# Moving side splits, side sums and weight sums to other places of a hand-written order in a fused attention and bilinear-GLU kernel

## The chip, the cores and the metric

The kernel runs on one core of a Trainium2 chip. A core has a matrix engine (PE, whose weight loads the profile lists apart as PEld), a vector engine (DVE), a scalar engine (ACT), GpSimd (POOL) and a queue engine (SP) that issues the DMA transfers. Each engine works through its own instructions in the order in which the program issues them, and semaphores make one wait for another. The metric is the device time of one execution in microseconds. A difference of 0.2%, about 1.07 us here, is the smallest that is called a difference.

## The reference, cut to what matters

```python
mod = (silu(c) @ w_mod).reshape(1, 6, 1, -1)          # shifts, scales and gates sa, ca, ga, sb, cb, gb
h = layernorm(x) * (1 + ca) + sa
x = x + ga * linear_attention(h, A_wqkv, A_wo)
h = layernorm(x) * (1 + cb) + sb
g = h @ B_w_gate                                       # 2048 x 512 by 512 x 1376
u = h @ B_w_up
x = x + gb * ((g * u) @ B_w_down)                      # 2048 x 1376 by 1376 x 512
```

All tensors are float32. The change is in the last three lines: the feed-forward part behind the second layer norm.

## The kernel before, in words

**Precision.** A float32 operand is split in two parts, a high part `h` (the value rounded to the matrix engine's format) and a low part `l = x - h`. A product is three matrix products: `h*h`, `h*l` and `l*h`. The helper `split` does it: ACT writes `h` (line 202), and DVE, or POOL where `low` names it, writes `l` (line 203). So every low part is a DVE instruction behind an ACT instruction.

**Chunks and sides.** The 2048 tokens are cut in four chunks of 512. The gate and up projections of two chunks at a time are done by a Strassen-Winograd scheme with seven products in place of eight. The 2x2 block matrix on the left has the two chunks as rows and the two halves of the 512 features as columns. Its sides are the blocks `a11`, `a12` (first chunk of the pair), `a21`, `a22` (second chunk) and the sums `s1 = a21 + a22`, `s3 = a11 - a21`, `s2 = s1 - a11`, `s4 = a12 - s2` (`Left.sum`, line 1059, on DVE). Each half of the features is two tiles of 128 rows, so each side comes twice, for `k` = 0 and 1. The seven products use `a11, s1, s2, a12, s3, s4, a22`, each split in `h` and `l`.

**Steps and places.** One call of `block` is one step: one tile of 128 columns of gate and up for one pair of chunks. Steps 0 to 7 work on the first and second chunk, steps 8 to 18 on the third and fourth. A step has seven products of six matmuls each (`times`, line 1150), 42 matmuls of 128x512, and after each product a place where other work is put in: `p1` behind the product of `a11`, then `p5` (`s1`), `p6` (`s2`), `p2` (`a12`), `p7` (`s3`), `p3` (`s4`) and `p4` (`a22`), in this order. The four accumulators `a, b, c, d` are PSUM banks; steps from 3 on take the set named `bank` when they are even and the set named `acc` when odd. In each step ACT copies `a` to `b` behind the first product, `d` to SBUF behind the second, and `b` to `c` and to SBUF behind the third (line 1155). At the fifth product DVE adds accumulator `c` to a copy (line 1212), and the seventh product then adds on to the same `c`. So **the last six matmuls of a step may not start before the L1212 instruction of that step has read `c`**, and between the fifth and the seventh product lies only the sixth, six matmuls. L1216 and two L1178 follow on DVE in the same step.

**What sets the order around it.** The order is written out by hand. Two tables fill the places of the steps. One is the dictionary near the end of the main function: it holds the work on the third and fourth chunk that steps 8 and later need, namely `flips` (DVE block transposes, line 344, into the one buffer `wide`), `turned` (ACT, line 349, makes a block from `wide`), `sums` and `split_in`. The other is `Down.planned`: the weights of the down projection, in pairs `i` of row tiles. For each even step 8, 10, 12, 14 and 16 it scales the pair by `gb` (`w_scale`, line 1326, two DVE instructions), makes the four Winograd sums `t1` to `t4` (`w_sum`, line 1340, four DVE instructions of 128x256, both inputs in SBUF) and splits the parts (`w_parts`, lines 1318 and 1319). POOL has its own load in steps 2 to 11: at `p4` of a step it makes four sums of the next gate and up weights (line 1094), and at `p7`, behind four ACT instructions (lines 1105 and 1108), the four low parts of the next step's weights (line 1112). All DMAs named here are issued by SP.

## Time and profile before

| what | value |
|---|---|
| median of 3 runs | 536.81 us (536.5 to 537.18) |
| the profiled execution, device time | 537.02 us |
| its span, first to last instruction | 535.3 us |
| granted matrix clock | 1.00 of full speed, throughout |
| moved by DMA | 113.41 MB, mean 212 GB/s |

Between the span and the device time of the same execution lie 1.7 us at the ends. The steps 3 to 18 stand in the span from 282.28 us on, at some 9.5 us each. In the rows below a row gives its start in us from the start of the span, its length in us, the engine, the line, the instruction, output<-inputs, the size, and in square brackets how long the engine had been idle before it and for whom it had waited. A row that ends in x2 is two instructions that follow each other without a gap.

### The profile page before, as it was taken

Reading aid. Unit: us, or ns where it says so; the run is one execution under the profiler, and the core shown is the slowest. Engines: PE = TensorE matmul, PEld = TensorE weight load, DVE = VectorE, ACT = ScalarE, POOL = GpSimd, SP = SyncE. Lnnn points to the kernel's source line nnn. Section 1 sums busy time; section 2 is a strip of 40 time slices with the busy share of each in tenths; the row PEclk is TensorE's granted clock in tenths of the full one; section 3 lists DMA queues with packets and bytes.
Section 4 is the critical chain, followed back from the end, with each engine's and each line's share of the span. In section 5 each row is a group of like instructions: output and inputs, shape, how many; then the busy total and the mean of one; then the engine's idle time right before and its main releaser. Section 6 shows DMA issues by size and latency. Waiting matters only on the chain.

```text
span 535.3 us, 8162 instructions
## 1 busy us (share of the span) xinstructions
PE 527.9 (99%) x2551; PEld 440.9 (82%) x2551; DVE 416.4 (78%) x732; ACT 312.3 (58%) x588; POOL 143.3 (27%) x141
## 2 busy tenths in 40 slices
PE   8999999999999999999999999999999999999997
PEld 7888888888878878878888878678888889998887
DVE  7997879999999888779645697777477677788594
ACT  3696878759577774576584853563424454425530
POOL 2001010000012220076587894591001244100000
PEclk9999999999999999999999999999999999999999
DMA  8912426220065155957979965297999789969866
GB/s 276 387 45 79 158 95 212 89 79 2 32 209 182 55 202 156 282 164 212 297 246 308 334 258 149 82 337 254 370 334 326 257 313 335 290 226 278 254 158 153
DMA packets 102203, 113.41 MB, mean 212 GB/s; under 512 B 26448, under 2 KB 57168, under 8 KB 102160
## 3 DMA queue, kind: packets, MB, share of 16 engines
q1 hardware_dynamic: 97808, 111.85, 63.9%
q10 hardware_dynamic: 4352, 1.05, 0.9%
q8 instruction: 20, 0.33, 0.3%
q14 instruction: 23, 0.19, 0.1%
HBM read 70.91 MB, written 41.94 MB: 211 GB/s over the span
## 4 chain that ended last, share of the span: by engine, by line
PE 96%; DVE 1%; POOL 1%; DMA 1%; issue 0%; ACT 0%; POOLq 0%
PE bank L1150 17%; PE acc L1150 14%; PE acc L882 8%; PE acc L1413 6%; PE bank L216 4%; PE bank L217 4%; PE bank L215 4%; PE acc L1434 4%; PE bank L1434 4%; PE bank L1413 3%; PE acc L424 3%; PE acc L423 3%; PE acc L422 3%; PE bank L967 2%; PE bank L965 2%; PE bank L966 2%
## 5 line engine op out<-in xcount | busy, mean ns | idle before, releaser
L1150 PE MATMUL bank<-h,w 128*128 128x512 f32 x462 | 107.3, 390 | 2.1 <-DVE u L1212 2.1
L1150 PEld LDWEIGHTS bank<-h,w 128*128 128x128 f32 x462 | 86.5, 188 | 21.3 <-DVE u L1212 3.4
L1150 PE MATMUL acc<-h,w 128*128 128x512 f32 (+1 forms) x336 | 77.8, 390 | 0.0
L1150 PEld LDWEIGHTS acc<-h,w 128*128 128x128 f32 (+1 forms) x336 | 61.9, 184 | 14.6 <-DVE u L1212 0.3
L271 POOL TENSOR_TENSOR rstd<-ve,half 128x2 f32<-128x2 f32 (+3 forms) x13 | 11.9, 912 | 108.7 <-DVE ve L270 45.7
L1155 ACT ACTIVATE bank<-bank 128x512 f32<-128x512 f32 x24 | 14.0, 582 | 46.1 <-PE bank L1150 41.5
L215 PE MATMUL bank<-w,h 128*128 128x512 f32 x104 | 40.6, 391 | 0.0
L217 PE MATMUL bank<-w,h 128*128 128x512 f32 x104 | 40.6, 390 | 0.0
L216 PE MATMUL bank<-w,h 128*128 128x512 f32 x104 | 40.5, 390 | 0.0
L882 PE MATMUL acc<-w,xh 128*128 128x512 f32 x120 | 37.4, 392 | 0.0
L1155 ACT ACTIVATE acc<-acc 128x512 f32<-128x512 f32 (+1 forms) x18 | 10.5, 581 | 42.8 <-PE acc L1150 31.4
L1413 PE MATMUL acc<-w,kh 128*128 128x256 f32 (+1 forms) x176 | 31.9, 283 | 0.0
L1112 POOL TENSOR_TENSOR w<-raw,w 128x256 fp32r<-128x256 f32 (+3 forms) x22 | 24.6, 1118 | 24.6 <-ACT w L1105 24.6
L1112 POOL TENSOR_TENSOR w<-t,w 128x512 fp32r<-128x512 f32 (+1 forms) x22 | 31.1, 1415 | 0.0
L1413 PEld LDWEIGHTS acc<-w,kh 128*128 128x128 f32 (+1 forms) x176 | 27.6, 192 | 0.2
L882 PEld LDWEIGHTS acc<-w,xh 128*128 128x128 f32 x120 | 22.4, 188 | 5.1 <-DVE w L793 0.3
L422 PE MATMUL acc<-kh,xh 128*128 128x512 f32 x64 | 25.1, 392 | 0.0
L424 PE MATMUL acc<-kl,xh 128*128 128x512 f32 x64 | 25.0, 390 | 0.0
L423 PE MATMUL acc<-kh,xl 128*128 128x512 f32 x64 | 24.9, 390 | 0.0
L1413 PE MATMUL acc<-w,kl 128*128 128x256 f32 x88 | 24.9, 283 | 0.0
L202 ACT ACTIVATE kh<-u 128x512 fp32r<-128x512 f32 (+1 forms) x38 | 21.0, 623 | 5.6 <-PE acc L1413 3.0
L203 DVE TENSOR_TENSOR kl<-u,kh 128x512 fp32r<-128x512 f32 (+1 forms) x28 | 17.6, 685 | 7.8 <-ACT kh L202 7.8
(267 smaller groups left out, 1342.0 us busy)
## 6 DMA issues: line engine op xcount, KB each, us to landing
right<-w SPq DMA_DIRECT2D x49, 256.0 KB, 3.2
w<-right SPq DMA_DIRECT2D x49, 256.0 KB, 5.1
w<-down_t SPq DMA_DIRECT2D x36, 256.0 KB, 5.3
w<-down_b SPq DMA_DIRECT2D x27, 256.0 KB, 4.6
raw<-in_w_mod_dram SPq DMA_DIRECT2D x24, 256.0 KB, 4.2
down_t<-w SPq DMA_DIRECT2D x20, 256.0 KB, 4.7
x<-in_A_x_dram SPq DMA_DIRECT2D x16, 256.0 KB, 5.4
x<-x SPq DMA_DIRECT2D x16, 256.0 KB, 4.4
```

The lines of the kernel that those rows point to most:

```text
L215: nc.tensor.matmul(ps, ah, bh, start=i == 0, stop=False)
L216: nc.tensor.matmul(ps, ah, bl, start=False, stop=False)
L217: nc.tensor.matmul(ps, al, bh, start=False, stop=i == n - 1)
L422: nc.tensor.matmul(tacc[k], xh[:, a:b], kh, start=first, stop=False)
L423: nc.tensor.matmul(tacc[k], xl[:, a:b], kh, start=False, stop=False)
L424: nc.tensor.matmul(tacc[k], xh[:, a:b], kl, start=False, stop=last)
L882: nc.tensor.matmul(yps[i], x, y, start=False, stop=k == KD - 1 and x is al, skip_group_check=True)
L1112: sub = lambda out, x, y: (on or nc.gpsimd).tensor_tensor(out, x, f32(y), op=ALU.subtract)
L1150: mm = lambda x, y, **kw: nc.tensor.matmul(ps, x[:, k], y, skip_group_check=True, **kw)
L1155: nc.scalar.activation(out, x, AF.Copy)
L1413: nc.tensor.matmul(ps, x[:, a:b], y, start=start, stop=False, skip_group_check=True)
L1434: nc.tensor.matmul(ps, of[:, x], y, start=start, stop=False, skip_group_check=True)
```

## The change

Part one is in `Down.planned`: the sums `t1, t2` go from place `p2` to `p5` of the even steps, and `t3, t4` from `p3`, where they stood behind the splits of `b11` and `b21`, to `p6`. Part two is the dictionary: the splits of the third chunk's `a11` (both `k`) and of its `a12` for `k` = 0 go into step 3, beside the flips of the fourth chunk; `turned` of the fourth chunk moves one place or more ahead in step 4; and the sums and the splits of the sums, which stood in steps 5 to 7, are spread over steps 4 to 7. The split of the second `a22` goes from `p6` to `p1` of step 8. No instruction is added or taken away, and SP and POOL keep the order of what they do; their buffers come in another turn.

```diff
-                put(a, "p2", lambda i=i: self.w_sum(i, "t1", "t2"))
-                put(a, "p3", lambda i=i: self.w_parts(i, "b11", "b21"), lambda i=i: self.w_sum(i, "t3", "t4"))
+                put(a, "p5", lambda i=i: self.w_sum(i, "t1", "t2"))
+                put(a, "p6", lambda i=i: self.w_sum(i, "t3", "t4"))
+                put(a, "p3", lambda i=i: self.w_parts(i, "b11", "b21"))
                 put(a, "p4", lambda i=i: self.w_parts(i, "b22", "t1"))
...
-        (3, "p1"): [turned(1, 2, "a12")], (3, "p6"): [flips(3, 0)], (3, "p2"): [flips(3, 1)],
-        (3, "p3"): [flips(3, 2)], (3, "p4"): [flips(3, 3)],
-        (4, "p5"): [turned(0, 3, "a21"), split_in(0, "a11")], (4, "p6"): [split_in(0, "a12")], (4, "p2"): [turned(0, 3, "a22")],
-        (4, "p3"): [turned(1, 3, "a21"), split_in(1, "a11")], (4, "p4"): [turned(1, 3, "a22")],
-        (5, "p1"): [sums(0, "s1")], (5, "p5"): [split_in(1, "a12")], (5, "p6"): [sums(0, "s3")], (5, "p2"): [split_in(0, "s1")],
-        (5, "p3"): [sums(1, "s1")], (5, "p4"): [split_in(0, "s3"), sums(1, "s3")],
-        (6, "p1"): [sums(0, "s2")], (6, "p5"): [split_in(1, "s1")], (6, "p2"): [split_in(0, "s2"), sums(1, "s2")],
-        (6, "p3"): [split_in(1, "s3")], (6, "p4"): [sums(0, "s4")],
-        (7, "p1"): [split_in(1, "s2")], (7, "p6"): [sums(1, "s4")], (7, "p2"): [split_in(0, "s4")],
-        (7, "p3"): [split_in(1, "s4")], (7, "p4"): [split_in(0, "a22")], (8, "p6"): [split_in(1, "a22")]}.items():
+        (3, "p1"): [turned(1, 2, "a12")], (3, "p5"): [split_in(0, "a11")], (3, "p6"): [flips(3, 0)],
+        (3, "p2"): [flips(3, 1), split_in(0, "a12")], (3, "p3"): [flips(3, 2)], (3, "p4"): [flips(3, 3), split_in(1, "a11")],
+        (4, "p1"): [turned(0, 3, "a21")], (4, "p5"): [turned(0, 3, "a22")], (4, "p6"): [split_in(1, "a12"), sums(0, "s1")],
+        (4, "p2"): [turned(1, 3, "a21"), sums(0, "s3")], (4, "p3"): [turned(1, 3, "a22")],
+        (4, "p4"): [split_in(0, "s1"), sums(1, "s1")],
+        (5, "p5"): [sums(1, "s3")], (5, "p6"): [split_in(0, "s3")], (5, "p2"): [sums(0, "s2")],
+        (5, "p3"): [split_in(1, "s1")], (5, "p4"): [sums(1, "s2")],
+        (6, "p1"): [split_in(0, "s2")], (6, "p6"): [sums(0, "s4")], (6, "p2"): [split_in(1, "s3")], (6, "p4"): [split_in(1, "s2")],
+        (7, "p1"): [sums(1, "s4")], (7, "p5"): [split_in(0, "s4")], (7, "p2"): [split_in(1, "s4")],
+        (7, "p4"): [split_in(0, "a22")], (8, "p1"): [split_in(1, "a22")]}.items():
```

The order on DVE shows where this matters. A row is the line, the instruction, output<-inputs and the size. The first place is step 4 up to its last accumulator read; `f` are blocks of the third and fourth chunk, `s` sums, `h` low or high parts, and L1212 reads accumulator `c` (`bank_2883`). Before:

```order
L203 TENSOR_TENSOR h_3413<-f_3269,h_3412 128x512
L203 TENSOR_TENSOR h_3426<-f_3279,h_3425 128x512
L1212 TENSOR_TENSOR u_3408<-bank_2883,u_3408 128x512
L1216 TENSOR_TENSOR u_3423<-bank_2884,u_3423 128x512
L1178 TENSOR_TENSOR u_3423<-bank_2881,u_3423 128x512
```

And in the changed kernel:

```order
L203 TENSOR_TENSOR h_3404<-f_3294,h_3403 128x512
L203 TENSOR_TENSOR h_3436<-f_3303,h_3435 128x512
L1059 TENSOR_TENSOR s_3439<-f_3414,f_3424 128x512
L1059 TENSOR_TENSOR s_3463<-f_3269,f_3414 128x512
L1212 TENSOR_TENSOR u_3422<-bank_2883,u_3422 128x512
```

The two splits ahead of L1212 are those of another `k`, and two sums of sides have come in between them and L1212.

The second place is DVE between the last accumulator read of step 5 (`acc_3183`) and L1212 of step 6 (`bank_2883`). Before:

```order
L1178 TENSOR_TENSOR u_3523<-acc_3183,u_3523 128x512
L203 TENSOR_TENSOR h_3610<-s_3538,h_3609 128x512
L1059 TENSOR_TENSOR s_3613<-f_3294,f_3487 128x512
L1059 TENSOR_TENSOR s_3622<-s_3515,f_3269 128x512
L203 TENSOR_TENSOR h_3633<-s_3594,h_3632 128x512
L203 TENSOR_TENSOR h_3666<-s_3622,h_3665 128x512
L1059 TENSOR_TENSOR s_3669<-s_3594,f_3294 128x512
L1212 TENSOR_TENSOR u_3630<-bank_2883,u_3630 128x512
```

And in the changed kernel:

```order
L1178 TENSOR_TENSOR u_3535<-acc_3183,u_3535 128x512
L1059 TENSOR_TENSOR s_3621<-s_3520,f_3294 128x512
L203 TENSOR_TENSOR h_3631<-s_3572,h_3630 128x512
L1059 TENSOR_TENSOR s_3651<-f_3279,s_3572 128x512
L203 TENSOR_TENSOR h_3674<-s_3537,h_3673 128x512
L1212 TENSOR_TENSOR u_3640<-bank_2883,u_3640 128x512
```

Six side instructions stood there, four stand there now; the others have gone to steps 4, 5 and 7.

The third place is DVE in step 10, the second step with weight sums; `raw` are the weights of the down projection, `row_1578` is `gb`, `t` holds the sums, `w` their low parts. Before:

```order
L1326 TENSOR_TENSOR raw_4004<-raw_4004,row_1578 128x512
L1340 TENSOR_TENSOR t_4054<-raw_4002 128x256
L1340 TENSOR_TENSOR t_4054<-raw_4004,t_4054 128x256
L1212 TENSOR_TENSOR u_4029<-bank_2883,u_4029 128x512
L1216 TENSOR_TENSOR u_4038<-bank_2884,u_4038 128x512
L1178 TENSOR_TENSOR u_4038<-bank_2881,u_4038 128x512
L1319 TENSOR_TENSOR w_4088<-raw_4002,w_4088 128x256
L1319 TENSOR_TENSOR w_4091<-raw_4004,w_4091 128x256
L1340 TENSOR_TENSOR t_4055<-raw_4004,raw_4002 128x256
L1340 TENSOR_TENSOR t_4055<-raw_4004,t_4054 128x256
```

And in the changed kernel:

```order
L1326 TENSOR_TENSOR raw_4004<-raw_4004,row_1578 128x512
L1340 TENSOR_TENSOR t_4031<-raw_4002 128x256
L1340 TENSOR_TENSOR t_4031<-raw_4004,t_4031 128x256
L1340 TENSOR_TENSOR t_4032<-raw_4004,raw_4002 128x256
L1340 TENSOR_TENSOR t_4032<-raw_4004,t_4031 128x256
L1212 TENSOR_TENSOR u_4029<-bank_2883,u_4029 128x512
```

The two sums that stood behind L1212 and the splits now stand ahead of L1212. The same holds in steps 8, 12, 14 and 16.

## The prediction

> **What bounds the kernel now.** The first view is the page, busy time by engine.

> ```profile
> PE 527.9 (99%) x2551; PEld 440.9 (82%) x2551; DVE 416.4 (78%) x732; ACT 312.3 (58%) x588; POOL 143.3 (27%) x141
> ```

> PE is busy for 99% of the span and so the bound almost everywhere, and the change takes no matmul away. It can only gain where PE waits, and only lose by making PE wait. The second view is busy time by stretch, cut at the first matmul of each step (steps 3, 4, 5, 6, 8, 10 and 11; first the stretch, its length, then each engine's busy time with its count).

> ```profile
> 282.28:291.80 9.52, 9.52 (x44) 7.88 (x43) 3.99 (x7) 4.85 (x9) 7.53 (x9) 1.00 0.92 320
> 291.80:301.33 9.53, 9.53 (x44) 7.87 (x42) 5.32 (x9) 7.20 (x14) 6.26 (x8) 1.00 1.03 348
> 301.33:311.05 9.72, 9.72 (x44) 7.81 (x43) 8.37 (x11) 6.92 (x14) 9.64 (x9) 1.00 0.98 340
> 311.05:322.13 11.08, 9.82 (x44) 7.80 (x42) 11.05 (x13) 5.81 (x11) 11.00 (x9) 1.00 0.52 198
> 331.65:342.32 10.67, 9.82 (x44) 7.78 (x42) 8.00 (x13) 5.56 (x13) 4.46 (x5) 1.00 0.02 8
> 351.98:361.80 9.82, 9.82 (x43) 7.81 (x42) 7.76 (x12) 6.37 (x14) 9.74 (x9) 1.00 1.00 344
> 361.80:371.32 9.52, 9.52 (x43) 7.88 (x42) 6.83 (x14) 3.21 (x7) 1.71 (x2) 1.00 0.66 233
> ```

> A step without a wait is 9.52 us at a granted clock of 1.00. Step 6 loses 1.56, step 8 loses 1.15, step 10 loses 0.30, step 5 loses 0.20. The timeline of PE names the cause in the two longest:

> ```profile
> 320.63 1.66 PE L1150 MATMUL bank<-h,w 128*128 128x512 f32 x6 [1.26 <-DVE u L1212]
> 340.82 1.66 PE L1150 MATMUL bank<-h,w 128*128 128x512 f32 x6 [0.85 <-DVE u L1212]
> ```

> It is the last product of the step, six matmuls, waiting for L1212. L1212 in steps 5 and 6, the two low parts ahead of it in step 6, a low part with POOL idle, and a row of POOL for later:

> ```profile
> 308.81 0.68 DVE L1212 TENSOR_TENSOR u<-acc,u 128x512 f32<-128x512 f32 x1
> 316.45 2.37 DVE L203 TENSOR_TENSOR h<-s,h 128x512 fp32r<-128x512 f32 x2
> 319.90 0.68 DVE L1212 TENSOR_TENSOR u<-bank,u 128x512 f32<-128x512 f32 x1
> 333.08 0.68 DVE L203 TENSOR_TENSOR h<-f,h 128x512 fp32r<-128x512 f32 x1
> 299.14 0.74 POOL L1112 TENSOR_TENSOR w<-raw,w 128x256 fp32r<-128x256 f32 x1 [1.28 <-ACT w L1105]
> ```

> In step 6 DVE is busy for 11.05 of 11.08 us and POOL for 11.00 (the row by stretch), and a low part that takes 0.68 alone takes 2.37/2, about 1.2, there: the two take turns. L1212, whose one input is in PSUM, keeps its 0.68.

> **A rule for one step.** The last product is due 36 of 42 matmuls into the step, 9.52 x 36/42 = 8.16. Loss = (end of L1212) - (start of step + 8.16) + 0.19 fits all four: step 5, 309.49 - 309.49 + 0.19 = 0.19 (0.20 in the row); step 6, 320.58 - 319.21 + 0.19 = 1.56; step 8, 340.77 - 339.81 + 0.19 = 1.15; step 10, 360.26 - 360.14 + 0.19 = 0.31 (0.30). The ends of steps 8 and 10 come from rows below. So L1212 has to start by 7.29 into the step.

> **The change part by part.** *Step 6.* Two of six side instructions leave, about 2.4 us. The last one left ahead of L1212 is a low part behind an ACT high part; that comes behind two ACT copies, about 5.9 into the step, and even at 1.2 is over at about 7.1. Then L1212 waits for its own accumulator only. **-1.56.**

> *Step 8.* Here the wait was a DVE gap:

> ```profile
> 333.21 0.58 ACT L1155 ACTIVATE bank<-bank 128x512 f32<-128x512 f32 x1 [4.16 <-PE bank L1150]
> 337.56 0.69 DVE L203 TENSOR_TENSOR h<-f,h 128x512 fp32r<-128x512 f32 x1 [2.60 <-ACT h L202]
> 340.09 0.68 DVE L1212 TENSOR_TENSOR u<-bank,u 128x512 f32<-128x512 f32 x1
> 337.86 0.86 POOL L1112 TENSOR_TENSOR w<-raw,w 128x192 fp32r<-128x192 f32 x1 [8.04 <-ACT w L1105]
> ```

> DVE sat 2.60 us for the high part of the second `a22`, which stood at `p6`. At `p1` it follows the copy at 333.21, 3 us earlier, and then the low part and all four weight sums run in a stretch where POOL is idle until 337.86: about 334.4 + 0.6 + 4 x 0.35 = 336.4, long before L1212 can start at 338.7. **-1.15.** The bound on the other side is nothing gained.

> *Step 10.* The same edit meets another neighbour:

> ```profile
> 354.79 1.35 DVE L203 TENSOR_TENSOR kl<-u,kh 96x512 fp32r<-96x512 f32 x2 [1.80 <-ACT kh L202]
> 356.06 1.82 DVE L1326 TENSOR_TENSOR raw<-raw,row 128x512 f32<-128x512 f32 x2
> 357.81 0.96 DVE L1340 TENSOR_TENSOR t<-raw 128x256 f32<-128x256 f32 x1
> 358.81 0.85 DVE L1340 TENSOR_TENSOR t<-raw,t 128x256 f32<-128x256 f32 x1
> 359.58 0.68 DVE L1212 TENSOR_TENSOR u<-bank,u 128x512 f32<-128x512 f32 x1
> 361.78 2.01 DVE L1319 TENSOR_TENSOR w<-raw,w 128x256 fp32r<-128x256 f32 x2
> 363.71 0.41 DVE L1340 TENSOR_TENSOR t<-raw,raw 128x256 f32<-128x256 f32 x1
> 354.95 2.39 POOL L1094 TENSOR_TENSOR t<-raw,raw 128x256 f32<-128x256 f32 x1
> 359.34 1.47 POOL L1112 TENSOR_TENSOR w<-t,w 128x512 fp32r<-128x512 f32 x1
> 360.77 1.30 POOL L1112 TENSOR_TENSOR w<-raw,w 128x512 fp32r<-128x512 f32 x1
> ```

> DVE starts late because its first low parts wait for high parts behind the first product, and L1212 has no slack (0.30 lost). Two more L1340 now come at 359.58. POOL then holds a 128x512 low part from about 359.5 to 360.76. The third sum waits for it and ends reading at 361.1; POOL's next one has taken the turn, to 362.2; the fourth sum is over at 362.56, and L1212 ends at 363.24 in place of 360.26. **+2.98.** That a short DVE instruction waits out a long POOL one is in the row at 361.78: two instructions that take 0.41 each alone (363.71) took 2.01, as POOL's 128x512 at 360.77 and the next ran. Bounds: 0.70 (two at 0.35 without a wait) and 2.98; I take the upper, to which that row is nearest.

> *Steps 12, 14, 16.* DVE waits for PE before L1212 there; the smallest gap of the three:

> ```profile
> 416.47 0.69 DVE L1212 TENSOR_TENSOR u<-bank,u 128x512 f32<-128x512 f32 x1 [1.76 <-PE bank L1150]
> ```

> Two sums of 0.35 fit into 1.76: **0**. Without that cover it would be 0.7 for each.

> *Step 4.* The rows that time ACT and POOL there (the first is the copy behind the third product, one step earlier):

> ```profile
> 286.56 0.58 ACT L1155 ACTIVATE acc<-acc 128x512 f32<-128x512 f32 x1 [0.76 <-PE acc L1150]
> 298.65 0.41 ACT L1105 ACTIVATE w<-raw 128x256 fp32r<-128x256 f32 x1
> ```

> Now a low part and two sums stand ahead of L1212. The low part needs its ACT high part behind the two copies of the third product; the first of these comes 4.28 into a step (286.56 in the step that starts at 282.28), so at 296.08, and the high part, two ACT instructions later at 0.5 each, is done by 297.67. Low part to 298.3, first sum to 298.9, at 0.6 each. ACT's L1105 comes about 0.38 earlier than at 298.65, since one instruction less holds up the third product's copies, and POOL's L1112 0.49 behind it as before (299.14), at 298.76; so the second sum waits until 299.48 and is over at 300.05; L1212 ends at 300.73. Loss 300.73 - 299.96 + 0.19 = 0.96 against 0.01: **+0.95**. Bounds: +0.40 if the second sum meets no POOL instruction, +0.95.

> *Step 5.* Five side instructions stand ahead of L1212 where four stood; by the same count, taking turns with POOL, the last sum starts behind the low part of `s3` and L1212 ends 0.17 past due: loss 0.36 against 0.20, **+0.16** (0 to 0.7).

> *Steps 3 and 7.* Step 3 takes three low parts and three ACT high parts. It has 3.99 us of DVE work in 9.52 us, and two flips and two low parts, 2.6 us, fit behind ACT's copies and ahead of L1212; step 7 has four side instructions as before: **0**. *DMA and queues.* No transfer moves in SP's order; buffers come free in another turn, but every DVE, ACT and POOL instruction that waits for a transfer does so behind one that, by the landings before, is over by more than a microsecond, or for the same weight loads as before. **0**, with up to a few tenths if one is late.

> Sum: 0.95 + 0.16 - 1.56 - 1.15 + 2.98 = **+1.38**, on the profiled execution's 537.02 (span 535.3), so 538.4. The median is 0.21 lower, 536.81, which makes **538.2**.

> [...] While POOL's instruction begun at 354.95 stood for 2.39, DVE ran three two-input instructions unhindered: the two at 354.79 took 1.35, and the first at 356.06 its plain 0.68 of the 1.82. [...]

> **The rivals.** (1) *Strict turns.* If that free passage is not repeated in step 10, DVE comes to the sums later by one or two POOL instructions, about 1.1 us: 538.2 + 1.1 = **539.3**. For it: turns were kept in nearly every other meeting. Against: the same instructions meet in the same place. (2) *DVE keeps going in step 10.* If the two added sums pass without waiting for POOL, as the three at 354.79 did, step 10 costs 0.70 in place of 2.98: 538.2 - 2.3 = **535.9**, not slower; the point from which it decides is one passage, since with one wait it is 537.2. With step 4 at its lower bound it is 535.4, faster. (3) *The early steps hide.* If the sums of steps 4 and 5 meet no POOL instruction, 0.95 + 0.16 falls to 0.40: **537.5**. That the edit does not do what it says would need step 6 or 8 to wait as before: 1.2 to 1.6 more, within the upper range with (3).

> **How the numbers follow.** Forecast 0.55, (1) 0.13, (2) 0.20, (3) 0.12. About 0.2% (1.07 us) is what a measurement of this kernel can tell from no change. The forecast lies 0.3 above that bound and its terms are good to about 0.4, so 0.42 of its 0.55 is slower and 0.13 within; (1) is slower; (2) is half faster, half within; (3) is within. Slower 0.55, same 0.35, faster 0.10. The range from 535.8 to 539.5 leaves out the faster half of (2) and the far end of (1).

> **What would show it.** In the changed profile: steps 6 and 8 at 9.52 us with no PE wait; step 10 near 12.8 us with the largest PE wait for L1212 of the kernel, ahead of it four L1340 of which the last two take about 1.5 each; step 4 near 10.5 us. Wrong would be: no wait in step 10, or two L1340 rows at 0.41 there; a wait left in step 6 or 8; any wait of PE for something other than L1212 in steps 3 to 8, such as an ACT copy or a DMA.

## The result, and the profile after

| | median | lowest to highest |
|---|---|---|
| before | 536.76 us | 536.50 to 537.18 (6 runs) |
| after | 540.34 us | 539.34 to 541.20 (6 runs) |

The ratio is 1.0066, with a 95% interval from 1.0053 to 1.0079: the changed kernel is slower by 3.6 us, where 1.4 was forecast, and the time lies above the forecast's range. The profiled execution of the changed kernel is its longest run, 541.20 us (span 539.5), 4.18 us above the profiled one of before.

The page of the changed kernel, busy time by engine, and the row of the granted matrix clock in 40 slices of 13.5 us:

```profile
PE 530.6 (98%) x2551; PEld 442.6 (82%) x2551; DVE 412.6 (76%) x732; ACT 312.3 (58%) x588; POOL 141.3 (26%) x141
PEclk9999999999999999999999999988999999999999
```

PE is busy for 530.6 us where it was 527.9, with the same 2551 matmuls: these have become longer. Two slices, at 350 to 377 us, show a granted clock below 90%. Before, no slice did. The busy time by stretch, cut at the first matmul of steps 4, 5, 6, 8, 10 and 11 (the stretch, its length, busy time and count for PE, PEld, DVE, ACT and POOL, then the granted clock, the DMA share and GB/s):

```profile
291.78:302.34 10.56, 9.81 (x43) 7.81 (x42) 7.10 (x11) 8.05 (x14) 8.29 (x9) 1.00 1.04 364
302.34:312.25 9.91, 9.81 (x43) 7.81 (x42) 8.07 (x10) 5.17 (x10) 9.18 (x9) 1.00 0.98 345
312.25:321.77 9.52, 9.52 (x43) 7.88 (x42) 7.09 (x9) 5.71 (x11) 9.26 (x9) 1.00 0.36 138
331.30:340.82 9.52, 9.52 (x44) 7.86 (x42) 6.58 (x13) 5.59 (x13) 3.83 (x5) 1.00 0.00 2
350.48:364.34 13.86, 11.08 (x43) 8.72 (x42) 11.27 (x15) 6.36 (x14) 11.54 (x10) 0.88 0.73 252
364.34:375.54 11.20, 11.20 (x43) 9.05 (x42) 4.27 (x9) 3.21 (x7) 0.00 (x0) 0.85 0.91 317
```

Against the rows of before: step 4 +1.03, step 5 +0.19, step 6 -1.56, step 8 -1.15, step 10 +4.04, step 11 +1.68. The sum is +4.23, which is the whole difference of the two executions. Steps 4 to 8 did what was forecast; steps 10 and 11 hold the rest. The timeline of PE there, and of DVE ahead of L1212 in step 10:

```profile
350.48 8.35 PE L1150 MATMUL bank<-h,w 128*128 128x512 f32 x36
361.62 2.92 PE L1150 MATMUL bank<-h,w 128*128 128x512 f32 x6 [2.78 <-DVE u L1212]
364.34 11.36 PE L1150 MATMUL acc<-h,w 128*128 128x512 f32 x42
```

```profile
358.06 1.50 DVE L1340 TENSOR_TENSOR t<-raw,raw 128x256 f32<-128x256 f32 x1
359.49 1.48 DVE L1340 TENSOR_TENSOR t<-raw,t 128x256 f32<-128x256 f32 x1
360.89 0.68 DVE L1212 TENSOR_TENSOR u<-bank,u 128x512 f32<-128x512 f32 x1
```

DVE earlier in the step, and POOL beside it and beside the two L1340:

```profile
353.22 1.41 DVE L203 TENSOR_TENSOR kl<-u,kh 96x512 fp32r<-96x512 f32 x2 [1.74 <-ACT kh L202]
354.55 1.82 DVE L1326 TENSOR_TENSOR raw<-raw,row 128x512 f32<-128x512 f32 x2
353.44 2.39 POOL L1094 TENSOR_TENSOR t<-raw,raw 128x256 f32<-128x256 f32 x1
357.82 1.46 POOL L1112 TENSOR_TENSOR w<-t,w 128x512 fp32r<-128x512 f32 x1
359.25 1.44 POOL L1112 TENSOR_TENSOR w<-raw,w 128x512 fp32r<-128x512 f32 x1
```

The wait for L1212 is there, 2.78 us long, behind two L1340 of 1.5 each, and each of these two ends 0.28 behind a POOL instruction that it overlaps. But the last product, six matmuls, then takes 2.92 where 1.66 is normal, and step 11, which waits for nothing, takes 11.36 where 9.68 is normal. Stretches of the same trace cut ever finer find where the clock changes:

```profile
350.48:358.83 8.35, 8.35 (x37) 6.57 (x35) 6.58 (x9) 6.16 (x14) 8.27 (x8) 1.00 1.01 341
358.83:360.98 2.15, 0.01 (x1) 0.00 (x0) 2.15 (x3) 0.20 (x1) 2.15 (x3) 1.00 0.64 245
360.98:367.80 6.82, 6.18 (x15) 4.83 (x16) 3.90 (x8) 0.58 (x1) 1.11 (x1) 0.50 0.42 151
367.80:375.54 7.74, 7.74 (x35) 6.37 (x34) 2.91 (x6) 2.62 (x6) 0.00 (x0) 1.00 0.98 341
```

PE stands idle from 358.83; at 360.98, still idle, its clock falls to half, and it comes back at 367.80. In between PE is busy for 6.18 us at half speed. Step 10 and step 11 together are +5.72. A last product that had to wait stands 1.50 ahead of the next step at full clock (320.63 to 322.13 in the kernel before), so before it started 9.82 - 1.50 = 8.32 into step 10, and now it starts at 11.14: the wait is +2.82, and the clock the rest, +2.90. Had the clock stayed, step 10 would have been 12.64 us long and the execution 541.20 - 2.90 = 538.3. The expectation of `weights_only` below puts the wait at +2.68; the run itself, whose step 10 was 12.64 us long at full clock, bears out +2.82.

### The profile page after: what moved, and what is told of

The parts are those of the page before. It is cut to its first block, busy times and chain, and to the rows that moved or that the text cites. A ratio compares the mean times of both kernels' runs of the same rounds, so it can differ in the third digit from the quotient of the medians.

```text
span 539.5 us, 8159 instructions
## 1 busy us (share of the span) xinstructions
PE 530.6 (98%) x2551; PEld 442.6 (82%) x2551; DVE 412.6 (76%) x732; ACT 312.3 (58%) x588; POOL 141.3 (26%) x141
## 4 chain that ended last, share of the span: by engine, by line
PE 94%; DMA 2%; DVE 1%; SPq 1%; POOL 1%; issue 1%; ACT 0%; DVEq 0%; POOLq 0%
PE bank L1150 18%; PE acc L1150 13%; PE acc L882 8%; PE acc L1413 6%; PE bank L216 4%; PE bank L217 4%; PE bank L215 4%; PE acc L1434 4%; PE bank L1434 4%; PE bank L1413 3%; PE acc L424 3%; PE acc L423 3%; PE acc L422 3%; PE bank L967 2%; PE bank L965 2%; PE bank L966 2%
## 5 line engine op out<-in xcount | busy, mean ns | idle before, releaser
L1150 PE MATMUL bank<-h,w 128*128 128x512 f32 x462 | 108.2, 393 | 3.5 <-DVE u L1212 3.5
L1150 PEld LDWEIGHTS bank<-h,w 128*128 128x128 f32 x462 | 87.3, 189 | 22.6 <-DVE u L1212 4.4
L1150 PE MATMUL acc<-h,w 128*128 128x512 f32 (+1 forms) x336 | 79.6, 396 | 0.1
L1150 PEld LDWEIGHTS acc<-h,w 128*128 128x128 f32 (+1 forms) x336 | 63.2, 188 | 15.4 <-DVE u L1212 0.5
L1155 ACT ACTIVATE bank<-bank 128x512 f32<-128x512 f32 x24 | 14.0, 582 | 47.8 <-PE bank L1150 43.1
L1155 ACT ACTIVATE acc<-acc 128x512 f32<-128x512 f32 (+1 forms) x18 | 10.5, 581 | 47.9 <-PE acc L1150 36.4
L1112 POOL TENSOR_TENSOR w<-raw,w 128x256 fp32r<-128x256 f32 (+3 forms) x22 | 24.3, 1104 | 27.6 <-ACT w L1105 24.8
L1112 POOL TENSOR_TENSOR w<-t,w 128x512 fp32r<-128x512 f32 (+1 forms) x22 | 30.4, 1383 | 0.0
L882 PE MATMUL acc<-w,xl 128*128 128x512 f32 x60 | 23.6, 393 | 0.0
L202 ACT ACTIVATE kh<-u 128x512 fp32r<-128x512 f32 (+1 forms) x38 | 21.0, 622 | 4.4 <-PE acc L1413 3.0
```

Source lines behind the costliest of these rows:

```text
L882: nc.tensor.matmul(yps[i], x, y, start=False, stop=k == KD - 1 and x is al, skip_group_check=True)
L1112: sub = lambda out, x, y: (on or nc.gpsimd).tensor_tensor(out, x, f32(y), op=ALU.subtract)
L1150: mm = lambda x, y, **kw: nc.tensor.matmul(ps, x[:, k], y, skip_group_check=True, **kw)
L1155: nc.scalar.activation(out, x, AF.Copy)
```

## The experiments

Theory A: the wait of step 10 costs twice, first its length, then a granted clock that falls to half because PE stood idle. Rivals: the loss beyond the forecast comes with the dictionary, or with other sums or buffers, or the clock falls for another cause. The steps are numbered as above in the rows of every experiment.

### One part alone

`weights_only` is the kernel before with part one alone, `table_only` with part two alone.

> Only the weight sums moved (the rows of Down.planned), the dictionary as before. Theory A (the wait of step 10 costs twice: the wait itself, and the granted clock that falls to half behind it): step 6 stays 11.08 us, step 8 loses its 1.15 (the four sums fit into the DVE gap of 2.60 ahead of the low part), step 10 waits as in the changed kernel (+2.68 against before) and the clock falls to 0.5 behind it (+2.2 to +2.9): 536.8 - 1.15 + 2.68 + 2.2 to 2.9 = 540.5 to 541.2. Rival B (the loss beyond the forecast comes with the dictionary, from steps 3 to 8 and their buffers): no half clock, 536.8 - 1.15 + 2.68 = 538.3.

> Only the dictionary changed, the weight sums where they stood before. Theory A: steps 4 and 5 +1.03 and +0.19, steps 6 and 8 at 9.52 (-1.56, -1.15), step 10 at 9.82 as before, no stretch at half clock: 536.8 - 1.5 = 535.3. Rival B (the loss comes with the dictionary): 537.5 or more, with a stretch of lower clock or longer steps somewhere.

`weights_only` took 540.11 us (539.15 to 540.54), ratio 1.0056 [1.0043, 1.0068]; `table_only` 535.31 us (535.21 to 535.93), ratio 0.9969 [0.9959, 0.9980], where the kernel before took 537.01. The stretches of `weights_only` for steps 6, 8, 10 and 11, and for the one in which its clock was at half; behind the dots step 8 of `table_only`:

```profile
311.02:322.11 11.09, 9.81 (x44) 7.80 (x43) 11.05 (x13) 5.81 (x11) 11.01 (x9) 1.00 0.47 179
331.65:341.17 9.52, 9.52 (x43) 7.86 (x42) 7.26 (x14) 5.56 (x13) 3.31 (x4) 1.00 0.01 2
350.84:363.48 12.64, 9.84 (x43) 7.81 (x42) 10.83 (x14) 6.36 (x14) 11.54 (x10) 1.00 0.78 268
363.48:374.63 11.15, 11.15 (x43) 9.02 (x42) 4.62 (x11) 3.21 (x7) 0.00 (x0) 0.85 0.91 308
363.49:366.90 3.41, 3.41 (x10) 2.64 (x9) 1.70 (x5) 0.58 (x1) 0.00 (x0) 0.50 0.74 272
...
331.24:340.77 9.53, 9.53 (x44) 7.86 (x43) 5.92 (x11) 5.58 (x13) 3.83 (x5) 1.00 0.00 0
```

The two parts split as theory A has it: part one alone makes the kernel slower, and part two alone makes it faster. The weight sums of step 8 cost nothing, since they fill the DVE gap that stood there, and cure its wait without the dictionary. Step 10 waits as in the changed kernel (2.80 us), and the clock falls behind it, but this time only as step 11 begins, and for 3.41 us in place of 6.82, which costs 11.15 - 9.52 = 1.63. That is why the time lies below the 540.5 to 541.2 that was expected. One of the five runs, 539.15, shows a mean clock of 1.000: it was spared.

### The whole change without its sums in step 10

```diff
+                if i == 1:
+                    put(a, "p2", lambda i=i: self.w_sum(i, "t1", "t2"))
+                    put(a, "p3", lambda i=i: self.w_parts(i, "b11", "b21"), lambda i=i: self.w_sum(i, "t3", "t4"))
+                else:
...
```

> The whole change, but in step 10 alone the weight sums stand where they stood before. Theory A: the same as with the dictionary alone, since steps 12, 14 and 16 hide their sums: step 10 at 9.82, no half clock, 535.3. Rival C (the sums of steps 12, 14 and 16 or the order of buffers after them cost too): 536 or more, with waits in steps 12 to 16.

535.59 us (534.88 to 535.94), ratio 0.9974 [0.9963, 0.9984], not to be told from `table_only`. Step 10 and steps 12 and 16:

```profile
350.81:360.63 9.82, 9.82 (x43) 7.80 (x42) 7.82 (x12) 6.37 (x14) 9.74 (x9) 1.00 0.99 339
370.15:379.67 9.52, 9.52 (x43) 7.88 (x42) 6.48 (x13) 3.54 (x8) 0.00 (x0) 1.00 1.03 368
408.23:417.75 9.52, 9.52 (x43) 7.89 (x42) 7.72 (x15) 3.57 (x8) 0.00 (x0) 1.00 0.80 262
```

Step 14 is 9.52 us too. So the places of four instructions in one step hold all of the loss, 540.34 - 535.59 = 4.75 us, and the sums of steps 12 to 16 are free.

### The wait kept, the idle time filled

```diff
+    def filler(n):
+        for _ in range(n):
+            nc.tensor.matmul(others[0], ones_r, second_side["a11"][0][0], start=True, stop=True, skip_group_check=True)
+    plan.setdefault((10, "p3"), []).append(lambda: filler(12))
```

> The whole change, and 12 more matmuls of 128x512 behind the sixth product of step 10, whose result is overwritten unread: at 0.227 each they fill 2.72 us, about the whole wait of PE. Theory A (PE standing idle makes the clock fall): L1212 ends where it ends in the changed kernel, step 10 about 12.6 us, clock 1.00 throughout, 540.3 - 2.2 to 2.9 = 537.4 to 538.2. Rival D (the clock falls for another cause, such as what DVE and POOL do then, or by chance): 0.5 behind step 10 as before, 540.3 or more.

538.30 us (538.07 to 538.60), ratio 1.0022 [1.0012, 1.0032], 0.1 above the expected 537.4 to 538.2. Steps 10 and 11, and the added matmuls:

```profile
350.70:363.40 12.70, 12.59 (x55) 10.06 (x54) 10.89 (x14) 6.36 (x14) 11.62 (x10) 1.00 0.82 269
363.40:372.92 9.52, 9.52 (x43) 7.88 (x42) 4.62 (x11) 3.21 (x7) 0.00 (x0) 1.00 0.92 301
358.89 2.91 PE L1908 MATMUL acc<-h,ones_r 128*128 128x512 f32 x12
```

DVE and POOL do in step 10 what they do in the changed kernel (the last two L1340 take 1.52 and 1.51 us), and the step still ends 2.9 us late; but with twelve useless matmuls in the gap the clock stays at 1.00, step 11 is 9.52, and the kernel is 2.0 us faster than the changed one. All eight runs show a mean clock of 0.999 or 1.000. That settles the cause: it is PE's idle time that makes the clock fall, and neither the work of the other engines nor chance.

### POOL's instructions in halves

```diff
...
-                sub(l, x, h)
+                for i in range(2) if halves else ():
+                    sub(l[:, i], x[:, i], h[:, i])
+                if not halves:
+                    sub(l, x, h)
...
-            rights[n].lows(on)
+            rights[n].lows(on, halves=n == 11)
```

The halves are made for the weights of step 11 alone, which POOL prepares in step 10.

> The whole change, with the three low parts of 128x512 that POOL makes in step 10 cut into two of 128x256 each. If the last two sums of step 10 take 1.5 each because they wait out a POOL instruction: they take about 0.8 to 0.95 each, PE waits 1.4 to 1.7 in place of 2.78, and if so short an idle stretch keeps the clock as the 1.26 of before did, 540.3 - 1.2 - 2.2 = 536.9 (to 537.4); if the clock falls all the same, 539.1. If the sums are slow for another cause: rows of 1.5 as before, and 540.3.

537.22 us (536.69 to 537.71), ratio 1.0006 [0.9997, 1.0014]. The last two sums of step 10, L1212 and POOL beside them, then PE (the file has three lines more, so that 1340, 1212 and 1150 read 1343, 1215 and 1153):

```profile
357.84 0.96 DVE L1343 TENSOR_TENSOR t<-raw,raw 128x256 f32<-128x256 f32 x1
358.72 0.94 DVE L1343 TENSOR_TENSOR t<-raw,t 128x256 f32<-128x256 f32 x1
359.58 0.68 DVE L1215 TENSOR_TENSOR u<-bank,u 128x512 f32<-128x512 f32 x1
357.60 1.78 POOL L1112 TENSOR_TENSOR w<-t,w 128x256 fp32r<-128x256 f32 x2
359.34 1.59 POOL L1112 TENSOR_TENSOR w<-raw,w 128x256 fp32r<-128x256 f32 x2
```

```profile
350.26 8.35 PE L1153 MATMUL bank<-h,w 128*128 128x512 f32 x36
360.31 1.67 PE L1153 MATMUL bank<-h,w 128*128 128x512 f32 x6 [1.71 <-DVE u L1215]
361.82 9.71 PE L1153 MATMUL acc<-h,w 128*128 128x512 f32 x42
```

The DVE work is the same; only POOL's instructions are shorter, and the sums fall from 1.50 and 1.48 to 0.96 and 0.94. That they waited out POOL's instructions is thereby shown. And an idle stretch of 1.71 left the clock alone: step 11 takes 9.71 here where it took 11.36.

### How long may PE stand idle?

The `ladder` is the kernel before with DVE products that nobody reads, ahead of L1212 in steps 12, 14 and 16, where POOL does nothing.

```diff
+    def delay(n):
+        for _ in range(n):
+            nc.vector.tensor_tensor(wide[:, 0], gb, gb, op=ALU.mult)
+    for at, n in (((12, "p2"), 8), ((14, "p2"), 7), ((16, "p2"), 8)):
+        plan.setdefault(at, []).append(lambda n=n: delay(n))
```

> The kernel before, with 8, 7 and 8 DVE products of 128x512 that nobody reads put ahead of L1212 in steps 12, 14 and 16, where POOL stands idle: by 0.60 each PE should stand idle for about 1.5, 2.0 and 2.6 us. Theory A (a long enough idle stretch of PE makes the clock fall, whatever is around it): half clock behind step 16 at least, at most a part of the three behind step 12; 536.8 + 1.7 + 2.2 + 2.8 = 543.5 for the waits, plus 2 to 3 for each stretch at half clock, 545.5 to 549. Rival D (the idle time is not the cause): 543.5 and a clock of 1.00.

550.15 us (549.03 to 550.84), ratio 1.0241 [1.0225, 1.0258]: above what was expected, since each product took 0.72 and not 0.60, so that the waits are longer. Two of the four runs, the traced one among them, have a mean clock of 0.991, and two have 0.994, which is one fall less. PE at the three waits, and the stretches at half clock:

```profile
381.74 2.51 PE L1150 MATMUL bank<-h,w 128*128 128x512 f32 x6 [2.24 <-DVE u L1212]
405.27 2.21 PE L1150 MATMUL bank<-h,w 128*128 128x512 f32 x6 [2.59 <-DVE u L1212]
429.57 2.53 PE L1150 MATMUL bank<-h,w 128*128 128x512 f32 x6 [3.33 <-DVE u L1212]
```

```profile
382.28:385.70 3.42, 3.42 (x9) 2.65 (x8) 3.32 (x9) 0.00 (x0) 0.00 (x0) 0.50 0.60 226
406.18:409.59 3.41, 3.41 (x10) 2.64 (x9) 3.41 (x9) 0.00 (x0) 0.00 (x0) 0.50 0.41 154
430.07:433.49 3.42, 3.42 (x9) 2.64 (x9) 3.38 (x10) 0.00 (x0) 0.00 (x0) 0.50 0.30 66
```

The clock falls in the kernel before, in steps where the change cost nothing, behind waits of 2.24, 2.59 and 3.33 us, and each time for 3.41 us. The three falls are 23.90 and 23.89 us apart, seven times 3.413. In the changed kernel the clock falls at 360.98 and once more at 538.47, behind PE's last matmul: 177.49 us, 52 times 3.413; in `weights_only` at 363.49 and 537.57: 174.08 us, 51 times. So in these traces the clock changes at instants 3.413 us apart, whatever work lies between two of them.

`ladder_short` has 7, 6 and 6 products instead, and was traced twice.

> The kernel before, with 7, 6 and 6 unread DVE products ahead of L1212 in steps 12, 14 and 16, one less in 12 and 14 and two less in 16 than in the ladder: PE should stand idle for 1.5, 1.9 and 1.9 us. Theory A with a window (the clock is set at fixed instants 3.41 us apart, by how much of the window before PE stood idle, the limit lying between 1.70 and 1.91 us): never half clock behind step 12; behind 14 and 16 only if nearly the whole idle stretch lies in one window, so in some runs and not in others; each time it costs 1.7. Waits alone: 536.8 + 1.7 + 2.1 + 2.1 = 542.7; with none to two such windows 542.7 to 546.1. Rival E (a plain threshold on the length of the idle stretch): the same stretches in every run.

> The same kernel once more, for a second trace. With the window: the instants at which the clock may change lie elsewhere against the steps, so steps 14 and 16 may come out the other way; step 12 at full clock again. With a plain threshold: as in the first trace.

544.91 us (543.07 to 545.92), ratio 1.0138 [1.0121, 1.0155]; the four runs show mean clocks of 0.994, 0.997, 0.997 and 1.000 with 545.92, 544.66, 545.17 and 543.07 us, which are two falls, one, one and none. The second trace, 544.8 us, shows 0.997. PE in the first trace, and then in the second:

```profile
380.64 1.66 PE L1150 MATMUL bank<-h,w 128*128 128x512 f32 x6 [1.50 <-DVE u L1212]
401.84 2.76 PE L1150 MATMUL bank<-h,w 128*128 128x512 f32 x6 [1.86 <-DVE u L1212]
424.68 1.91 PE L1150 MATMUL bank<-h,w 128*128 128x512 f32 x6 [1.89 <-DVE u L1212]
```

```profile
381.22 1.66 PE L1150 MATMUL bank<-h,w 128*128 128x512 f32 x6 [1.51 <-DVE u L1212]
402.41 2.18 PE L1150 MATMUL bank<-h,w 128*128 128x512 f32 x6 [1.86 <-DVE u L1212]
425.24 1.66 PE L1150 MATMUL bank<-h,w 128*128 128x512 f32 x6 [1.88 <-DVE u L1212]
```

The same wait in step 16, 1.89 and 1.88 us, makes the clock fall in the first trace (1.91 for six matmuls, and 11.16 for the next step) and not in the second (1.66). In the second the clock had fallen at 403.32 behind step 14, so the instants lie at 403.32 + 6 x 3.413 = 423.80 and at 427.21: the wait, from 423.36 to 425.24, is cut into 0.44 and 1.44. In the first the fall is at 425.95, the window runs from 422.54, and the wait, from 422.79 to 424.68, lies in it whole. Step 14's wait of 1.86 us, shorter than both, lay in one window in both traces and made the clock fall in both. A plain threshold on the length of the wait is out.

### A version that beats both

`behind_l1212` is the whole change with what made L1212 late in steps 4, 5 and 10 put behind it.

```diff
-                put(a, "p5", lambda i=i: self.w_sum(i, "t1", "t2"))
-                put(a, "p6", lambda i=i: self.w_sum(i, "t3", "t4"))
+                put(a, "p3" if i == 1 else "p5", lambda i=i: self.w_sum(i, "t1", "t2"))
+                put(a, "p3" if i == 1 else "p6", lambda i=i: self.w_sum(i, "t3", "t4"))
...
-        (4, "p2"): [turned(1, 3, "a21"), sums(0, "s3")], (4, "p3"): [turned(1, 3, "a22")],
+        (4, "p2"): [turned(1, 3, "a21")], (4, "p3"): [sums(0, "s3"), turned(1, 3, "a22")],
...
-        (5, "p5"): [sums(1, "s3")], (5, "p6"): [split_in(0, "s3")], (5, "p2"): [sums(0, "s2")],
-        (5, "p3"): [split_in(1, "s1")], (5, "p4"): [sums(1, "s2")],
+        (5, "p5"): [sums(1, "s3")], (5, "p6"): [split_in(0, "s3")], (5, "p3"): [sums(0, "s2"), split_in(1, "s1")], (5, "p4"): [sums(1, "s2")],
```

> The whole change with three edits: the sum of the third side of step 4 and that of the second side of step 5 behind L1212 of their step, and all four weight sums of step 10 behind its L1212. Theory A (each instruction ahead of L1212 past its slack costs its own time, and step 10's wait costs twice): the 0.30 of step 10, the 1.03 of step 4 and the 0.36 of step 5 go, on top of the dictionary alone at 535.3: 533.6 to 534.3, no step from 3 to 18 over 9.7 but those of 96 columns. Rival B (the sums only wait somewhere else, behind L1212 they hold up the next step): 535 or more, with a wait in step 5, 6 or 11.

534.39 us (534.27 to 534.86), ratio 0.9956 [0.9944, 0.9969], just above the expected 533.6 to 534.3. Steps 4 and 5 are at 9.52 us; step 6 became 9.93 and step 11 9.68. So rival B is right in a small part: the side sum of step 5 pushes six side instructions into step 6, whose last one starts at 317.28, and L1212 is 0.4 late there.

`behind_l1212_b` moves one more split, and turns the order of step 10 behind its L1212; `behind_l1212_c` keeps the first and takes half of the second back.

```diff
-        (6, "p1"): [split_in(0, "s2")], (6, "p6"): [sums(0, "s4")], (6, "p2"): [split_in(1, "s3")], (6, "p4"): [split_in(1, "s2")],
+        (6, "p1"): [split_in(0, "s2")], (6, "p6"): [sums(0, "s4")], (6, "p3"): [split_in(1, "s3")], (6, "p4"): [split_in(1, "s2")],
...
```

At `p3` of step 10, `behind_l1212_b` has the parts of `b11` and `b21`, then the sums of `t1` and `t2`, then those of `t3` and `t4`; `behind_l1212_c` has the sums of `t1` and `t2` first, then the parts, then the sums of `t3` and `t4`.

> The kernel behind_l1212 (534.39) with two more edits: in step 6 the second split of s3 behind L1212, as step 7 has DVE gaps of 0.94 and 1.10, and in step 10 the parts of b11 and b21 ahead of the four sums, as before. Theory A (each wait is L1212's end by the rule of one step): step 6 back from 9.93 to 9.52 (-0.41), step 11 from 9.68 to 9.52 (-0.16): 533.8. Rival B (the split only makes step 7 late): 534.4, with a wait in step 7 or 8.

> behind_l1212_b with the order of step 10 mended: behind its L1212 first the sums of t1 and t2, then the parts of b11 and b21, then the sums of t3 and t4. If the 0.84 that step 11 lost there is ACT's copy behind the first product standing behind ACT's part of t1, which waits for the DVE sum (3.78 us): step 11 back to 9.68, step 6 stays 9.52, 534.44 - 0.68 = 533.8. If step 11 was late for another cause, such as the banks: 534.4 with 10.36 again.

`behind_l1212_b` took 534.44 us (534.35 to 535.07), ratio 0.9958 [0.9945, 0.9970], and gained nothing: step 6 fell to 9.52, but step 11 grew to 10.36. That is the time of rival B, but not its wait, since steps 7 and 8 stayed at 9.52. ACT in step 10 and 11 there:

```profile
356.00 1.08 ACT L1318 ACTIVATE w<-raw 128x256 fp32r<-128x256 f32 x3
360.86 0.44 ACT L1318 ACTIVATE w<-t 128x256 fp32r<-128x256 f32 x1 [3.78 <-DVE t L1340]
361.19 0.59 ACT L1155 ACTIVATE acc<-acc 128x512 f32<-128x512 f32 x1
```

ACT's part of `t1` waits 3.78 us for the DVE sum, and behind it in ACT's order stands the copy that step 11's third product needs. `behind_l1212_c` took 534.28 us (533.79 to 534.31), ratio 0.9944 [0.9931, 0.9958], with step 11 back at 9.69: the cause was that. The 533.8 that was expected was missed by 0.5, but the kernel before also took 0.45 more beside these runs (537.29) than beside those of `behind_l1212_b`. The intervals of `behind_l1212`, `b` and `c` overlap, so of the three only the traces say which is better.

## Why the prediction was wrong, point by point

**Steps 6 and 8** (-1.56 and -1.15): right, to the hundredth; both are 9.52 us. For step 8 the experiments add that either part cures it alone.

**Steps 4 and 5** (+0.95 and +0.16): right; measured +1.03 and +0.19. The rule "Loss = (end of L1212) - (start of step + 8.16) + 0.19" held.

**Step 10, the wait.** Right in mechanism and nearly in size. It was forecast that L1212 ends 363.24 - 351.98 = 11.26 into the step, behind two L1340 of about 1.5; it ended at 11.09, behind two of 1.50 and 1.48. At full clock the step takes 12.64 us (`weights_only`) where 12.8 was forecast, so the wait is +2.82, and the rule of one step held for it too (11.09 - 8.16 + 0.19 = 3.12 = 12.64 - 9.52). That the two sums wait out POOL's instructions is shown by `pool_in_halves`.

**Step 10, the price of the wait.** Here the prediction failed: "L1212 ends at 363.24 in place of 360.26. **+2.98**". It took a wait to cost its length. The rule of one step was fitted on four waits, the longest with 1.26 us of PE idle time, and used on one of 2.8, in which another thing happens: the granted clock falls to half for one window of 3.41 us or two, partly in a step that waits for nothing. One window cost 1.63 us in `weights_only`; the profiled execution of the changed kernel had two, and lost 2.90. The mean clocks of the six runs, 0.993 in that one and 0.996 or 0.997 in the others, are those of two windows (1 - 0.5 x 6.83/539 = 0.994) and of one (0.997), less up to 0.001 for the fall behind the last matmul. With the clock kept, `fill_wait` measured 538.30 us against the forecast of 538.2. The other terms, as measured, sum to +1.33 where the forecast had +1.38, each within 0.2 of its own. The missing term is thus +2.90 in the profiled run and about +1.6 in the other five. By these terms the five would take 539.7; they took 539.34 to 540.43, and where the 0.6 us between 539.7 and the median comes from stays open, since none of the five was traced. The prediction had the granted clock in its own rows, as 1.00 throughout, and no rival asked what would change it.

**The rivals.** (1), strict turns, is out: the instructions that passed POOL's 2.39 at 354.95 passed it again, at 353.44 in the changed kernel's rows. (2), DVE keeps going, is out by the rows of 1.5. (3), the early steps hide, is out by steps 4 and 5. (1)'s number, 539.3, was the nearest to the time, but for a reason that did not occur.

**The free passage.** The prediction took the row at 354.95 to come again in step 10, and it did: 1.41 and 1.82 us for four DVE instructions, of which three ran beside POOL's 2.39. The two late sums it took by the row at 361.78 instead, and they came so, at 1.50 and 1.48.

## What to carry to other kernels

In these runs a wait of PE, the busiest engine, had its length as its price only while it was short. The 1.71 us of `pool_in_halves` left the clock alone; a wait of which 1.86 us or more lay in one window of 3.41 us cost a window at half clock on top, or two (one cost 1.63 us in `weights_only`), in a place where no wait is seen. So compare the length of a predicted wait with the longest one that the profile shows at full clock, and treat anything longer as a separate case. And where several instructions with slack stand ahead of one that another engine waits for, put them behind it, but look at what the engine that reads their results has queued behind.

## What the runs showed of the hardware

**A cheap cover.** Twelve matmuls whose result nobody reads, in a gap that couldn't be closed, were worth 2.0 us (540.34 to 538.30).

**An odd length.** A DVE product of 128x512 that reads one operand twice and writes the same place again took 0.72 us in a row of its kind (seven in 5.05 us), where 0.60 had been expected from others of that size (in the kernel before, the L203 of 333.08 is followed by the next instruction at 333.68). The runs do not show why.
